# Chunked attention into a gated feed-forward layer on one core: idle products in the head, 32-row value loads, three more tiles transposed by DMA

## The chip, the core and the metric

The program runs on one core of one Trainium2 chip. The core has TensorE (PE: matrix products), VectorE (DVE), ScalarE (ACT), GpSimd (POOL) and SyncE (SP). In this kernel GpSimd issues nearly all loads, SyncE a few small loads and the transposing transfers, ScalarE the stores. The metric is the device time of one execution in microseconds; 248.0 is the median of three runs (247.66 to 248.37). "Span" is the profiled part of one execution.

## The reference

There are 4 batches, 8 heads, 768 positions, head dimension 64. Positions are taken in chunks of 32. The queries of a chunk see 8 memory keys of their head and the keys from 16 positions before the chunk to 8 after it:

```python
for c in range(nc):                       # nc = 24 chunks per batch
    l_start = max(0, c_start - 16); r_end = min(S, c_end + 8)
    k_full = concat([mem_k, k[:, :, l_start:r_end]]); v_full = concat([mem_v, v[...]])
    a = softmax(q_c @ k_full.T / sqrt(D))
    out[:, :, c_start:c_end] = a @ v_full
x = out.transpose(0, 2, 1, 3).reshape(B * S, H * D)      # 3072 x 512
y = (relu(x @ w_gate) * (x @ w_val)) @ w_out             # 512 -> 1536 -> 512
```

All inputs and the output are float32. The kernel casts in the loads and computes in 16-bit types with float32 sums.

## The kernel before

**Tiles and blocks.** A tile is 128 positions of one batch, all heads: 24 tiles, 6 per batch. Attention runs tile by tile. The feed-forward layer runs over blocks of tiles (`BLOCKS = [2, 2, 2, 4, 4, 4, 4, 2]`): a first layer of 12 chunks, each with a gate product `g_ps` and a value product `v_ps` (line 396; four matmuls of 128 x 128 by 128 x 256 or 512), a relu on ScalarE (line 402), a multiplication on VectorE into `gvT` (line 408), and then the out products (line 421), copied and stored by ScalarE.

**One attention tile.** q and k are loaded as bfloat16 and transposed: batch 0 as pairs of tiles from `qk_p` (line 225), later tiles by TensorE (line 264), and from tile `LATE_QK = 18` on by a transposing transfer that SyncE issues (line 272). TensorE's transposes end in PSUM and are copied to `qT` and `kT` by ScalarE or VectorE (lines 78 and 80). Then scores (line 298, 32 small matmuls), row maximum, subtraction, exponent, row sum, reciprocal and normalising (lines 311 to 341). The probabilities are transposed by TensorE (line 347) and copied, or, from tile `LATE_P = 18` on, by SyncE's transfers (line 351). The product with the values is line 370 for batch 0 and line 377 for the other batches, its result is copied to `xT`.

**Values.** In batch 0 the value rows are loaded in natural order (`v_n`) and shifted to chunk order by products with a band matrix (`vs_ps`, line 204), then copied into `v_q`, a part of `v_bd[0]`. From batch 1 on the values stand in `v_bd[b % 2]`, a tile with 128 partitions in which each chunk has 56 context rows and 8 memory rows for each of two halves, and zeros elsewhere. The zeros are four GpSimd memsets of 128 x 1536 words per set (line 129): set 1 early (`z 1`), set 0 after batch 0. Two loads per batch (line 173) bring 56 rows of each of 96 chunks, so that rows shared by neighbouring chunks are fetched twice; eight small transfers bring the memory rows (line 156).

**What sets the order.** The program is written out by a list scheduler at the end of the kernel (`schedule()`, lines 660 to 757): operations with a cost per engine, dependencies, priorities and buffer counts (`room`). It gives each engine a fixed order, which the chip then runs in order. Loads are issued in the order of the list `loads`. PSUM buffers are `fps` (4, feed-forward and shifts), `sps` (1, scores) and `aps` (2, transposes and attention outputs). The planner multiplies some TensorE costs by 1.8 before 20 us.

Of the kernel before, what the change touches and what calls it, by code (L numbers as in the profile page):

```python
# [9 lines left out]
F32 = mybir.dt.float32  # L10
F16 = mybir.dt.float16
BF16 = mybir.dt.bfloat16
# [7 lines left out]
def kernel(  # L20
# [12 lines left out]
    nc = tc.nc  # L33
# [42 lines left out]
    def copy(eng, o, i):  # L76
        if eng is nc.scalar:
            nc.scalar.copy(o, i)  # L78
        else:
            eng.tensor_copy(o, i)  # L80
# [14 lines left out]
    vmem_f = v_bd[1][:, HP - 1].rearrange("p c d -> p (c d)").bitcast(F32)[:, 0:HP * 2 * D].rearrange(  # L95
        "p (h d) -> p h d", h=HP)
    v_q = v_bd[0][:, 0:2].rearrange("p h c d -> p (h c d)").rearrange("p (h c d) -> p h c d", h=HP, d=D)
    v_n = {}
# [27 lines left out]
        )  # L126

    def zero(eng, t, hp):
        eng.memset(t[:, hp].rearrange("p c d -> p (c d)").bitcast(F32), 0.0)  # L129


    def mem_load():
# [37 lines left out]
    def load_v_rows(b, par, s0, s1, c0, c1):  # L170

        dst = v_bd[b % NSET].rearrange("p h c d -> p (h c) d")
        nc.gpsimd.dma_start(  # L173
            dst[64 * par + s0:64 * par + s1, c0:c1, D * par:D * par + D],
            bass.AP(tensor=v.tensor, offset=v[b, HP * par, 0, 0].offset + (CH * c0 + s0 - 16) * D,
                    ap=[[D, s1 - s0], [CH * D, c1 - c0], [1, D]]))

    def v_parts(b, par, c0, c1):
        parts = []
        if (b, par, c1) == (B - 1, 1, HP * NCH):  # L180
            c1 -= 1
            parts.append((b, par, 0, 48, c1, c1 + 1))
        return parts + [(b, par, 0, CTX, c0, c1)]


    def load_v_tile(t):
# [21 lines left out]
    def shift_copy(c0, eng):  # L208
        copy(eng, v_q[:, :, c0:c0 + 2, :].rearrange("p h c d -> p c h d"), TMP.pop(("sh", c0)))
# [292 lines left out]
    for a in range(NT):  # L502
# [41 lines left out]
        if b == 0:  # L544
            for c0 in (4 * t, 4 * t + 2):
                need = {c // 4 for c in (c0, c0 + 1)} | {max(c0 - 1, 0) // 4, min(c0 + 2, NCH - 1) // 4}
                gone = ([t - 1] if c0 % 4 == 0 and t else []) + ([t] if c0 == NCH - 2 else [])
                op(("sh", c0), {"PE": 0.4}, lambda e, c0=c0: shift(c0), [("vn", n) for n in sorted(need)] + ["ident"],
                   (1, a, 7.5), ["fps"], ["qk"] * len(gone), [("s", t)])
                op(("shc", c0), psum(2 * HP * D), lambda e, c0=c0: shift_copy(c0, engine[e]), [("sh", c0)],  # L550
                   (1, a, 7.6), (), ["fps"])
# [39 lines left out]
    def load_qk_op(a, i):  # L591
        load(("qk", a, i), 1024, 1.05, lambda: load_qk(a, i), take=["qk"])

    def load_v_op(b, half, par, c0, c1, n, deps, after):
        for i, part in enumerate(reversed(v_parts(b, par, c0, c1))):
            rows = part[3] - part[2]
            load(("vl", b, half, n) if i == 0 else ("vx", b, n), rows * (part[5] - part[4]),
                 rows * (part[5] - part[4]) * 1.15e-3, lambda part=part: load_v_rows(*part), deps, (), after)

    def load_w_op(g):  # L600
        for w in range(2):
# [1 line left out]
                load(("w", g, w, par), 256, 0.35 * (GROUPS[g][1] - GROUPS[g][0]), lambda g=g, w=w, par=par: load_gate_val(g, w, par))  # L603

    def load_zero(s, hp):
        load(("z", s, hp), 0, 1.5, lambda: zero(nc.gpsimd, v_bd[s], hp), ["vm0"] if s else [("v", TPB - 1)])

    def load_pair_op(r, i):
        load(("pl", r, i), 1024, 1.45, lambda: load_pair(r, i))
# [27 lines left out]
    for i in range(2):  # L637
        load(("wo", i), 768, 4.1, lambda i=i: load_out(i))
    for b in range(1, B):
        deps = [("z", b % NSET, HP - 1)] + ([("v", TPB * (b - NSET + 1) - 1)] if b > NSET else [])  # L640
        if b == 1:
            for n in range(2 * HP):
                op(("mr", b, n), {"SP": 0.72}, lambda e, n=n: mem_rows(nc.sync, 1, n),
                   deps + [(("vm", 0), 0.2), (("vm", 1), 0.2)], (0,))
        for par in range(2):
            load_v_op(b, 0, par, 0, HP * NCH, par, [], deps)
        if b > 1:
            for n in range(2 * HP):
                load(("mr", b, n), 192, 0.22, lambda b=b, n=n: mem_rows(nc.gpsimd, b, n),
                     deps + [(("vm", 0), 0.2), (("vm", 1), 0.2)])  # L650
        for a, i in late[5 if b == 1 else 9 + 12 * (b - 1):21 + 12 * (b - 1)]:
            load_qk_op(a, i)
        if b == 1:
            for hp in range(HP):
                load_zero(0, hp)

    def timed(d):
        return isinstance(d, tuple) and len(d) == 2 and isinstance(d[1], float)

    def schedule():  # L660
        done, started, times = {}, set(), [0.7]
        free = {e: 0.7 for e in ("PE", "ACT", "DVE", "SP", "POOL")}
        queue_end, flying, gives = 0.0, [], []
# [26 lines left out]
        while len(started) < len(ops) + len(loads):  # L690
# [8 lines left out]
            while moved:  # L699
                moved = False  # L700
                for e in ("POOL", "PE", "ACT", "DVE", "SP"):
# [18 lines left out]
                    else:  # L720
                        o = None
                        for _, key in todo[e]:
                            late_pe = e == "PE" and t > 36.0 and ops[key]["prio"][0] == 1
                            if ready(ops[key], t, MARGIN if late_pe else 0.0):
                                o = ops[key]
                                break
                        if o is None:
                            continue
# [62 lines left out]
```

## Time and profile before

| | |
|---|---|
| median of three runs | 248.0 us |
| the profiled execution | 247.81 us |
| its span | 246.0 us |
| TensorE busy | 233.3 us, 95% |
| VectorE, ScalarE, GpSimd busy | 132.7, 117.6, 90.6 us |
| first first-layer product | 22.24 us from the span's start |
| last out product ends | near 242.2 us |

How to read it. Times are microseconds from the start of the span. In an instruction row the columns are start, duration, engine, line, operation, output and inputs, count, and in brackets the idle time before it and what ended it. Matmuls overlap each other, so four that take 0.6 us in such a row stand closer than 0.15 us; the chain of waits counts from start to start. A row of the chain is start, duration and what the time was spent on; "issue" is time in which the engine waited for nothing that the profile names. "POOL DMA_DIRECT2D" is GpSimd writing the descriptors of a load, not the load itself; "landing" is when its data has arrived. The row PEclk is the TensorE clock that was granted, in tenths of full speed.

### The profile page before, as it was taken

To read this page: it belongs to the slowest core of one execution; us is meant where nothing else is said; L and a number is where in the kernel's file an instruction comes from. 1 tells how busy PE (TensorE), PEld (TensorE's weight loads), DVE (VectorE), ACT (ScalarE), POOL (GpSimd) and SP (SyncE) were. 2 spreads that over 40 slices of the span, in tenths; PEclk is the share of its full clock that TensorE was granted. 3 is DMA by queue.
4 is the path that set the end of the run, shared out by engine and by line. 5 is a ranking of instruction groups with operands and counts; after the bars stand their busy time and mean duration, and the time that the engine had idled before them with its cause. 6 is when DMAs were issued, how large, how long until landed. Compare 5 with 4: busy or idle time off the path is not lost.

```text
span 246.0 us, 6397 instructions
## 1 busy us (share of the span) xinstructions
PE 233.3 (95%) x2673; PEld 139.8 (57%) x2673; DVE 132.7 (54%) x260; ACT 117.6 (48%) x265; POOL 90.6 (37%) x105
## 2 busy tenths in 40 slices
PE   0869999999999999999999999999999999999994
PEld 0646887884488645555445545555445444444873
DVE  2372757984139748796048779999342034320430
ACT  2755867753275445643245575765332232312432
POOL 8965799813268991099921050000000000000000
PEclk9999999999999999999999999999999999999999
DMA  7999999999999899999999999671101210002102
GB/s 74 173 179 203 203 96 119 174 175 127 133 223 154 80 102 136 75 75 147 179 192 158 67 76 109 130 147 25 23 0 45 85 44 0 0 35 95 43 3 85
DMA packets 109757, 25.76 MB, mean 105 GB/s; under 512 B 100769, under 2 KB 106657, under 8 KB 109729
## 3 DMA queue, kind: packets, MB, share of 16 engines
q0 software_dynamic: 94368, 16.42, 107.7%
q1 hardware_dynamic: 11760, 2.64, 8.9%
q10 hardware_dynamic: 3600, 6.29, 7.9%
q8 instruction: 21, 0.34, 0.6%
q14 instruction: 8, 0.06, 0.1%
HBM read 32.06 MB, written 6.29 MB: 156 GB/s over the span
## 4 chain that ended last, share of the span: by engine, by line
PE 92%; DMA 2%; DVE 2%; issue 1%; ACT 1%; POOL 1%; ACTq 0%; POOLq 0%
PE v_ps L396 26%; PE g_ps L396 26%; PE out_ps L421 25%; PE xT_ps L377 3%; PE s_ps L298 3%; PE qk_ps L264 2%; DMA qk_p<-in_k_dram 2%; PE pT_ps L347 2%; PE xT_ps L370 2%; PE vs_ps L204 1%; PE qk_ps L225 1%; PE xT_ps L363 1%; DVE mx L311 1%; POOL qk_p L216 1%; DVE dif L318 1%
## 5 line engine op out<-in xcount | busy, mean ns | idle before, releaser
L408 DVE TENSOR_TENSOR gvT<-v_ps,g_relu 128x256 f16<-128x256 f32 (+1 forms) x96 | 53.0, 555 | 56.7 <-PE v_ps L396 41.0
L396 PE MATMUL g_ps<-xT,w_gate_sb 128*128 128x256 f16 (+1 forms) x384 | 78.5, 327 | 0.0
L396 PE MATMUL v_ps<-xT,w_val_sb 128*128 128x256 f16 (+1 forms) x384 | 78.2, 326 | 0.0
L402 ACT ACTIVATE g_relu<-g_ps 128x256 f16<-128x256 f32 (+1 forms) x96 | 46.9, 489 | 50.7 <-PE g_ps L396 50.0
L421 PE MATMUL out_ps<-w_out_sb,gvT 128*128 128x512 f16 (+2 forms) x300 | 65.7, 371 | 0.0
L396 PEld LDWEIGHTS <-w_gate_sb 128*128 128x128 f16 x384 | 36.4, 98 | 24.0 <-issue 0.4
L396 PEld LDWEIGHTS <-w_val_sb 128*128 128x128 f16 x384 | 35.9, 98 | 20.9 <-issue 0.2
L421 PEld LDWEIGHTS <-gvT 128*128 128x128 f16 x300 | 28.0, 98 | 29.9
L78 ACT COPY o_sb<-out_ps 128x512 f32<-128x512 f32 (+2 forms) x25 | 14.2, 567 | 37.2 <-PE out_ps L421 28.2
L326 ACT ACTIVATE p_exp<-dif 128x256 f16<-128x256 f32 (+2 forms) x72 | 19.5, 336 | 9.0 <-DVE dif L318 8.8
L243 POOL DMA_DIRECT2D qk_b<-in_k_dram x18 | 16.5, 915 | 15.0 <-issue 8.4
L311 DVE TENSOR_REDUCE mx<-s_ps 128x8 f32<-128x512 f32 x24 | 16.5, 688 | 8.3 <-PE s_ps L298 8.0
L156 POOL DMA_DIRECT2D v_bd<-vmem x16 | 10.1, 642 | 27.7 <-DMA v_bd<-in_v_dram 27.7
L330 DVE TENSOR_REDUCE sm<-p_exp 128x8 f32<-128x512 f16 x24 | 16.4, 682 | 6.0 <-ACT p_exp L326 5.9
L78 ACT CAST xT<-xT_ps 128x512 f16<-128x512 f32 x19 | 11.1, 584 | 15.4 <-PE xT_ps L377 10.2
L243 POOL DMA_DIRECT2D qk_b<-in_q_dram x18 | 16.4, 913 | 3.1 <-issue 2.0
L341 DVE TENSOR_TENSOR p_n<-p_exp,rinv 128x512 f16<-128x512 f16 x24 | 16.5, 687 | 0.4
L318 DVE TENSOR_TENSOR dif<-s_ps,mx 128x512 f32<-128x512 f32 x24 | 16.4, 684 | 0.4
L173 POOL DMA_DIRECT2D v_bd<-in_v_dram x7 | 14.0, 2015 | 1.0 <-POOL v_bd L129 0.6
L377 PEld LDWEIGHTS <-v_bd 128*128 128x128 f16 x288 | 9.6, 96 | 4.7 <-issue 1.1
L78 ACT COPY kT<-qk_ps 128x512 bf16<-128x512 bf16 x17 | 10.8, 641 | 2.9 <-PE qk_ps L225 1.9
L129 POOL MEMSET v_bd<- 128x1536 f32 x8 | 10.7, 1397 | 0.0
(52 smaller groups left out, 156.8 us busy)
## 6 DMA issues: line engine op xcount, KB each, us to landing
out_dram<-o_sb ACTq DMA_DIRECT2D x23, 256.0 KB
v_bd<-in_v_dram POOLq DMA_DIRECT2D x5, 672.0 KB, 17.6
qk_b<-in_k_dram POOLq DMA_DIRECT2D x18, 128.0 KB, 6.1
qk_b<-in_q_dram POOLq DMA_DIRECT2D x18, 128.0 KB, 6.4
w_out_sb<-in_moe_w_out_dram POOLq DMA_DIRECT2D x2, 768.0 KB, 11.2
qk_p<-in_k_dram POOLq DMA_DIRECT2D x3, 256.0 KB, 5.2
qk_p<-in_q_dram POOLq DMA_DIRECT2D x3, 256.0 KB, 7.1
v_n<-in_v_dram POOLq DMA_DIRECT2D x6, 128.0 KB, 6.5
```

Source lines behind the costliest of these rows:

```text
L78: nc.scalar.copy(o, i)
L243: nc.gpsimd.dma_start(qk_b[a, i], bass.AP(tensor=x.tensor, offset=x[b, 0, 128 * t, 0].offset, ap=[[D, 128], [S * D, H], [1, D]]))
L311: nc.vector.reduce_max(SM[a, "mx"], s4, axis=AX.X)
L318: nc.vector.tensor_tensor(out=SM[a, "dif"].rearrange("p (m r) a s -> p r m a s", r=2), in0=S_ps.pop(a).rearrange("p r (m a) s -> p r m a s ...
L326: nc.scalar.activation(p[:, :, :, s0:s0 + k1 - k0], dif[:, :, :, k0:k1], ACT.Exp, scale=SCALE)
L330: nc.vector.reduce_sum(SM[a, "sm"], SM[a, "p"], axis=AX.X)
L341: nc.vector.tensor_tensor(out=P_n[a], in0=SM.pop((a, "p")), in1=rinv_b, op=ALU.mult)
L377: nc.tensor.matmul(ps[:, hp, r], lhsT=v_bd[b % NSET][:, hp, 4 * t + g, :], rhs=x[:, hp, r], start=True, stop=True)
L396: nc.tensor.matmul(ps, lhsT=w[:, f, 128 * m:128 * m + 128], rhs=xTs[blk][:, f, :], start=(f == 0), stop=(f == NFC - 1))
L402: nc.scalar.activation(st["r", m], st.pop((0, m)), ACT.Relu)
L408: nc.vector.tensor_tensor(out=st["gv"][:, m, :], in0=st.pop((1, m)), in1=st.pop(("r", m)), op=ALU.mult)
L421: nc.tensor.matmul(st["o", t, c], lhsT=st["gv"][:, m, 128 * t:128 * t + 128], rhs=w_out_sb[:, m, c[0]:c[1]], start=(m == 0), stop=(m == ND ...
```

## The change

Four things are changed.

1. **Idle products.** VectorE zeroes a 128 x 128 tile `idle` first of all. Wherever the scheduler finds TensorE with nothing ready between 1.3 and 16 us of its own time, it puts a product of that tile with itself into TensorE's order; nothing reads the results, which go to one `fps` buffer that is given back at 16.1. The order has 61 of them before the first k transposes (25 before and 36 behind the kmem product), then 7, 5, 7 and 5 between the first transposes, 22 before the scores of tile 1 and 31 before the first transposes of q pair 1. The factor of 1.8 now ends at 8 us.
2. **Early zeros.** Set 1 of `v_bd` is zeroed in the head, three quarters by VectorE (one before and two behind the identity copies) and one by ScalarE, which copies from `idle`; GpSimd's four memsets between the loads go. The scratch `vmem_f` moves to set 0. The shift copies of tiles 0 and 1 are fixed to ScalarE.
3. **Value loads of 32 rows.** The two loads of a batch bring rows 0 to 31 of each chunk, and a load of 16 rows the end of the last chunk. The rows 32 to 55 are copied on VectorE from the next chunk's rows 0 to 23: 16 copies per batch (24 partitions x 12 or 11 chunks x 64), first half of the batch and second half apart. The values of a tile wait for them.
4. **Transposing transfers** start at tile 15 instead of 18, for q and k and for the probabilities.

```diff
+    UT = 3
-    LATE_QK, LATE_P = 18, 18
+    LATE_QK, LATE_P = 15, 15
...
+    idle = const.tile([128, 128], BF16, name="idle")
...
     def zero(eng, t, hp):
-        eng.memset(t[:, hp].rearrange("p c d -> p (c d)").bitcast(F32), 0.0)
+        x = t[:, hp].bitcast(F32)
+        if eng is nc.scalar:
+            z = idle.bitcast(F32)
+            nc.scalar.copy(x, bass.AP(tensor=z.tensor, offset=z.offset, ap=[z.ap[0], [0, NCH], [1, D]]))
+        else:
+            eng.memset(x.rearrange("p c d -> p (c d)"), 0.0)
+
+    def idle_product(N):
+        if "idle" not in TMP:
+            TMP["idle"] = fps.tile([128, 512], F32, tag="fps", name="idle_ps")
+        nc.tensor.matmul(TMP["idle"][:, 0:N], lhsT=idle, rhs=idle[:, 0:N], start=True, stop=True)
...
+    def upper(b, par, i0, i1, eng):
+        x = v_bd[b % NSET].rearrange("p h c d -> p (h c) d")
+        d = slice(D * par, D * par + D)
+        copy(eng, x[64 * par + CH:64 * par + CTX, i0:i1, d], x[64 * par:64 * par + CTX - CH, i0 + 1:i1 + 1, d])
...
+    op("idle", {"DVE": 0.2}, lambda e: nc.vector.memset(idle, 0.0), prio=(-10,))
+    for hp in range(HP):
+        op(("z1", hp), {"DVE": 1.5, "ACT": 1.6}, lambda e, hp=hp: zero(engine[e], v_bd[1], hp), ["idle"], prio=(-1, hp), after=["warm2", "vmem_f"] + ["ib"] * (hp > 0))
...
-           + ([("vl", b, 0, n) for n in range(2)] if b else [("shc", 4 * t), ("shc", 4 * t + 2), "vm0"])
+           + ([("vl", b, n) for n in range(2)] + [("up", b, n, m) for n in range(2 * HP) for m in range(t // UT + 1)]
+              + [("ve", b, n) for n in range(2) if last] if b else [("shc", 4 * t), ("shc", 4 * t + 2), "vm0"])
...
+    def load_v_op(b, par, deps):
+        n = HP * NCH
+        load(("vl", b, par), CH * n, CH * n * 1.03e-3, lambda: load_v_rows(b, par, 0, CH, 0, n), (), (), deps)
+        load(("ve", b, par), 16, 0.05, lambda: load_v_rows(b, par, CH, CH + 16, n - 1, n), (), (), deps)
...
-    for hp in range(HP):
-        load_zero(1, hp)
...
+                            if e == "PE" and 1.3 < t < WARM:
+                                order.append((t, lambda: idle_product(128)))
+                                free[e] = t + (0.107 if t < 6.0 else 0.056)
...
-                        d *= (1.8 if e == "PE" and t < 20.0 and key[0] in ("t", "p", "sh", "f") else 1.0)
+                        d *= (1.8 if e == "PE" and t < 8.0 and key[0] in ("t", "p", "sh", "f") else 1.0)
```

More of the change, by code (lines that the diff above doesn't have):

```diff
@@ L94 @@
     v_bd = [const.tile([128, HP, NCH, 2 * D], F16, name=f"v_bd_{s}") for s in range(NSET)]
-    vmem_f = v_bd[1][:, HP - 1].rearrange("p c d -> p (c d)").bitcast(F32)[:, 0:HP * 2 * D].rearrange(
+    vmem_f = v_bd[0][:, HP - 1].rearrange("p c d -> p (c d)").bitcast(F32)[:, 0:HP * 2 * D].rearrange(
         "p (h d) -> p h d", h=HP)
@@ L592, in load_qk_op @@
         load(("qk", a, i), 1024, 1.05, lambda: load_qk(a, i), take=["qk"])
[L594 to L598, printed above, removed]
+    def load_v_op(b, par, deps):
+        n = HP * NCH
+        load(("vl", b, par), CH * n, CH * n * 1.03e-3, lambda: load_v_rows(b, par, 0, CH, 0, n), (), (), deps)
+        load(("ve", b, par), 16, 0.05, lambda: load_v_rows(b, par, CH, CH + 16, n - 1, n), (), (), deps)
+    for b in range(1, B):
+        for n in range(2 * HP):
+            hp, par = divmod(n, 2)
+            for m in range(TPB // UT):
+                i0 = NCH * hp + 4 * UT * m
+                i1 = min(i0 + 4 * UT, HP * NCH - 1)
+                op(("up", b, n, m), {"DVE": 0.1 + 64 * 0.5e-3 * (i1 - i0)},
+                   lambda e, b=b, par=par, i0=i0, i1=i1: upper(b, par, i0, i1, engine[e]),
+                   [("vl", b, par)], (1, TPB * b - 1 + 3 * m, 9) if b > 1 else (1, TPB * b - 1 + UT * m, -1), (), (), [("v", TPB * b - 7)] if b > 1 else [])
     def load_w_op(g):
@@ L605, in load_zero @@
     def load_zero(s, hp):
-        load(("z", s, hp), 0, 1.5, lambda: zero(nc.gpsimd, v_bd[s], hp), ["vm0"] if s else [("v", TPB - 1)])
+        load(("z", s, hp), 0, 1.5, lambda: zero(nc.gpsimd, v_bd[s], hp), [("v", TPB - 1)])
     def load_pair_op(r, i):
@@ L639 @@
     for b in range(1, B):
-        deps = [("z", b % NSET, HP - 1)] + ([("v", TPB * (b - NSET + 1) - 1)] if b > NSET else [])
+        deps = ([("z", 0, HP - 1)] if b > 1 else [("z1", hp) for hp in range(HP)]) + ([("v", TPB * (b - NSET + 1) - 1)] if b > NSET else [])
         if b == 1:
@@ L655 @@
                 load_zero(0, hp)
+    HASTE, WARM = 0.0, 16.0
     def timed(d):
@@ L662, in schedule @@
         free = {e: 0.7 for e in ("PE", "ACT", "DVE", "SP", "POOL")}
-        queue_end, flying, gives = 0.0, [], []
+        queue_end, flying, gives = 0.0, [], [(WARM + 0.1, "fps")]
+        room["fps"] -= 1
+        heapq.heappush(times, WARM + 0.1)
         todo = {e: [] for e in free}
@@ L726, in schedule @@
                                 break
+                            alone = len(ops[key]["eng"]) == 1 or e == "ACT"
+                            if e != "PE" and 6.0 < t < HASTE and alone and ready(ops[key], t + 0.4):
+                                break
                         if o is None:
+                            if e == "PE" and 1.3 < t < WARM:
+                                order.append((t, lambda: idle_product(128)))
+                                free[e] = t + (0.107 if t < 6.0 else 0.056)
+                                heapq.heappush(times, free[e])
+                            elif e == "PE" and t <= 1.3:
+                                heapq.heappush(times, 1.31)
                             continue
```

10 lines of the change are left out of this document (2 added, 8 removed).

## The prediction

> **What bounds the kernel now.** I read the page's busy times and slices first, then TensorE's instructions in order of time, then the chain of waits.
>
> ```profile
> span 246.0 us, 6397 instructions
> PE 233.3 (95%) x2673; PEld 139.8 (57%) x2673; DVE 132.7 (54%) x260; ACT 117.6 (48%) x265; POOL 90.6 (37%) x105
> ...
> PE   0869999999999999999999999999999999999994
> ...
> PEclk9999999999999999999999999999999999999999
> ...
> PE 92%; DMA 2%; DVE 2%; issue 1%; ACT 1%; POOL 1%; ACTq 0%; POOLq 0%
> ```
>
> TensorE is full from the third slice to the last. A gain is work taken off it, or an earlier start of that full stretch. The granted clock reads full everywhere, so TensorE's real rate must be read from durations:
>
> ```profile
> 12.42 1.49 PE L204 MATMUL vs_ps<-v_n,band 128*64 128x256 f16 x12
> 15.35 0.61 PE L347 MATMUL pT_ps<-band,p_n 128*128 128x128 f16 x4 [1.43 <-DVE p_n L341]
> 16.62 0.59 PE L363 MATMUL xT_ps<-pT,vmem 128*128 128x128 f16 x4 [0.67 <-ACT pT L78]
> 22.24 1.03 PE L396 MATMUL g_ps<-xT,w_gate_sb 128*128 128x256 f16 x4
> 23.55 1.36 PE L204 MATMUL vs_ps<-v_n,band 128*64 128x256 f16 x12
> 24.75 0.39 PE L225 MATMUL qk_ps<-ident_b,qk_p 128*64 128x128 bf16 x8
> 25.07 0.61 PE L396 MATMUL v_ps<-xT,w_val_sb 128*128 128x256 f16 x4
> ```
>
> Four 128x256 products took 1.03 us at 22.24 and 0.61 us at 25.07: until about 24.6 TensorE runs at half rate, though it was almost always busy from 6.2 to 13.9. The Trainium skill, "TensorE: Matmul & The Clock Gate", Part 1, says about 3.4 us of sustained matmuls open the gate; the trace disagrees, for those small products and transposes did not. Its Part 4, that transposes do not count as busy, agrees.
>
> ```profile
> 63.83 3.25 PE out_ps L421 x15
> 67.08 0.66 issue
> 67.74 1.06 PE xT_ps L377 x32
> ...
> 124.91 0.45 PE qk_ps L264 x8
> ...
> 144.07 0.22 PE qk_ps L264 x4
> ```
>
> This is the chain of waits: TensorE's costs from start to start, and its one pause after the head, 0.66 us before the values of tiles 6 and 7. The second v load of that batch was issued at 43.9 and landed 23.6 us later, at 67.5: it ended that pause.
>
> ```profile
> 84.22 2.21 POOL L173 DMA_DIRECT2D v_bd<-in_v_dram  x1 [0.57 <-POOL v_bd L129]
> 84.69 1.90 DVE L252 COPY kT<-kmemT 128x768 bf16<-128x768 bf16 x1
> 137.55 0.31 DVE L252 COPY kT<-kmemT 128x768 bf16<-128x768 bf16 x1
> ```
>
> The same VectorE copy took 0.31 us with GpSimd idle and 1.90 us under a GpSimd load, ending 0.16 us after it. Such copies are what the change adds.
>
> **The change, part by part.**
>
> *Idle products.* Nothing in the trace is a product of zeros; the nearest rows are the 128x128 products of L347: four in 0.61 us cold, one lasting 0.307, so 0.10 apart; four in 0.39 warm, so 0.055 apart. 61 stand before the first transposes: 25 (2.5 us from about 1.1) end before the kmem product at 4.21; 36 follow from 4.7 and end at 6.7 if the clock opens at once, 8.3 if it does not. The first k pair landed at 6.20, so they cost 0.5 to 2.1 us there; I take the middle, 7.2. From there to the scores of tile 0 lie one transpose group (0.6) and four ScalarE copies (0.66 each): about 10.5 against 9.71. The later products (7, 5, 7, 5, 22, 31) fill pauses; warm, 22 take 1.2 us and 31 take 1.7, beside the max-subtract-exp chain of 2.2 and 3.4 us, and are hidden; cold they would not be.
>
> *What ends the head then.* The order puts the first transposes of q pair 1 before P's transpose of tile 0. That load was issued at 9.76 and landed 7.1 to 7.6 us later; I take 17.2, a wait of TensorE that takes the place of the 1.43 us one. Behind it: transposes 0.28, P 0.39, VectorE's copy 0.42 (17.2 to 18.3); tile 0's second copy and values 0.83 (19.3); tile 1's reciprocal, normalise, P, copy beside these (20.3); values 0.83, ScalarE's copy 0.6 and the k transposes 0.57 beside it: the first-layer product starts at about 22.3. Before, it started at 22.31. But by then after has also done the scores (0.24), 12 shifts (0.78) and 8 transposes (0.22) that before did later: 1.24 us. And it meets no cold rows: before paid 0.53 extra for g (0.97 less 0.44), 0.10 for scores, 0.51 for the shifts (1.29 less 0.78): 1.14. Bounds for the start: 21.5 (landing 16.9, no waits between) to 23.3.
>
> *Dense start.* ScalarE must now give up four shift copies (0.59 each), k copies (0.64) and the first relus in the 4 us around the start, where cold TensorE used to leave time; the four fps buffers empty no faster. I charge 1.0 us (0 to 2).
>
> *Early zeros.* Two 128x1536 memsets follow ident_b on VectorE at 4.27. From the 128x512 row (0.485) each is at most 1.46, so the kT copy behind them ends at 7.5, or 9.1 if it waits like the 1.90 row. Scores at 10.5 cover it. ScalarE's zero (at most 3 x 0.584 = 1.75, from 2.24) ends before its 4.72 copy. If GpSimd's v loads are held up behind the memsets by up to 2.9 us, the DMA backlog (k landed at 9.1, first v at 10.05) hides most; the second v tile then costs up to 1 us, in the slack before 17.2. Price 0. On GpSimd 5.35 us of memsets go, and every load behind them is issued earlier.
>
> *Transposing transfers for tiles 15 to 17.* Six q/k groups of 0.22 and three P groups of 0.22 leave TensorE: 2.0 us. A following 128x512 group reads 0.97 instead of 0.86 after such a switch; about five switches fewer, 0.5. Together 2.5 (bounds 2.0 and 3.0). SyncE issues nine more, 1.2 to 1.9 us each, all behind its first at 112.77, before which it had waited 59.7 us: hidden. Its k_t copies replace PSUM copies of the same size (0.62 for 0.64 on ScalarE): no charge.
>
> *32-row v loads and copies.* Each load shrinks to 32/56. Before, the second landed 8.5 us after the first; at that ratio 4.9, and the first 3.1 instead of 5.4 behind w_out (landed 53.6). The five q/k loads ahead come about 3.1 us earlier (tile 8's k landed at 44.4; 35.5, the end of the backlog, plus 0.5 and five at 1.05 is 41.3). So the second v load lands near 53.6 - 3.1 + 3.1 + 4.9 = 58.5. Four copies then stand before tile 6's values: 0.31 each if free, 1.2 each if each waits for a 0.9 us GpSimd load: ready at 59.7 to 63.3. TensorE reaches these values after 24 out products, earlier than before: 22.3 + 31.3 (48 first-layer groups 20.9, scores 1.0, shifts 2.2, P and transposes 2.1, values 3.3, switches 1.8) + 6.1 (24 x 0.216, transposes, P, scores) + 1.0 above = 60.7. I take 61.5, a pause of 0.8 (0 to 2.6) for the 0.66 that goes. For batch 2, 16 copies join VectorE, busy 16.8 of 20 us from 90 to 110; I charge 0.4 (0 to 3). Batch 3's stand beside out products that need no VectorE. Behind a copy that waits for its load stand the gates; batch 2's and 3's loads come earlier than before, since GpSimd waited for v landings up to 67.5 and 104.3.
>
> The Trainium skill, "SBUF — State Buffer", section "SBUF: two separate sides", speaks against this part: a two-port VectorE operation and a GpSimd one exclude each other for a whole instruction. The 1.90 us row agrees. By it all copies beside loads cost 1.2 us, which is the third rival below.
>
> **The sum.** From 22.31 on, before spends 246.0 - 22.31 = 223.7 us. Take off 0.66, 1.14, 1.24 and 2.5: 218.1. After: 22.3 + 218.1 + 1.0 + 0.8 + 0.4 = 242.6 of span. Around the span lay 247.81 - 246.0 = 1.8 us; the profiled run lay 0.2 under the median of 248.0. Forecast: 244.4.
>
> **The rivals.**
>
> 1. *The added waits are all hidden.* For it: VectorE was busy only 3.8 of 12.3 us from 55.3 to 67.6. Then 22.3 + 218.1 + 1.8 = 242.2.
> 2. *The clock falls back when the idle products end,* in the 1.7 us pause before 17.2 and the thin work behind it, which in before never opened it. Price: values 2 x 0.8, shifts 0.6, k transposes 0.6 cold, then the 1.14 again, less the 1.0 of dense start: +2.9, 247.3, no change. Against it: after 24.6 no row slows again, though no pause there is longer than 0.66. By the clock page's rule only an idle window of about 3.4 us closes the gate, which would exclude this.
> 3. *Copies wait for GpSimd each time.* Tile 6's values wait 2.6 us, and 16 copies at 1.2 are 19 us of VectorE in a stretch with some 5 us to spare, so gates run late by about 3 us. 244.4 - 1.2 + 5.6 = 248.8, slower. It decides from about 0.9 us a copy. Against: loads are issued in bursts, and the 0.31 row.
> 4. *The change does not do what it says: products of zeros do not open the clock.* Then 36 cost 3.6 us, 22 and 31 cost 2.2 and 3.1 us cold, in the chain: scores at 11.7, P 10.5 us later at 22.2, first layer 7 us behind that (15.35 to 22.31 before) at 29.2. Plus 218.1 + 1.14 + 1.8: 250.2. Against it: a dense product is the only thing new just before 24.6.
>
> **How the numbers follow.** Forecast 0.53, rivals 0.22, 0.11, 0.08, 0.06. The forecast's own case covers 243 to 246. Range 241.7 to 248.2, leaving out the slow tails of 3 and 4 and a start below 22. A measurement of this kernel tells about 0.3% (0.7 us) from no change. Faster: 0.53 + 0.22 + a quarter of the second rival = 0.78; within: the rest of it, 0.08; slower 0.14.
>
> **What would show it.** Right: 0.055 us between idle products from about 6 to 8 us; 12 shifts in about 0.8 us before 16; a TensorE wait for q's load ending near 17.2; first-layer product near 22.3 at 0.61 for four; out products beginning near 54.5; values of tile 6 after a wait of under 1.5 us; the end at 240 to 244 of span. Wrong: 1.0 us for the first four 128x256 products, VectorE copies of 0.9 us or more before tile 6, a TensorE wait on gvT around 85 to 125, or waits for weights (w_val of chunk 6 landed near 29.7, needed at about 30.7).

## The result and the profile after

The changed kernel takes 254.92 us (median of four runs, 253.16 to 255.39); the kernel before took 248.19 in the same comparison. The ratio is 1.0264, 95% interval 1.0235 to 1.0293: slower by 2.6%. The forecast was 244.4 with a range of 241.7 to 248.2, so it had the wrong sign. (Ratios below leave out slow executions, one each of e4, e10 and e11 and four of ten of e9; of e8 five of six were slow, so it has no ratio, and the profiles of e8, e9 and e10 show slow executions.)

The page of the changed kernel, its busy times, slices and the shares of the chain of waits:

```profile
span 253.6 us, 6674 instructions
PE 240.0 (95%) x2775; PEld 145.8 (58%) x2775; DVE 160.1 (63%) x312; ACT 116.9 (46%) x260; POOL 83.1 (33%) x106
...
PE   7988799998929999999999999999999999999995
...
PEclk9999999999986999999999999999999999999999
...
PE 89%; DVE 3%; ACT 3%; issue 2%; DMA 1%; SPq 0%; ACTq 0%
```

A slice is 6.3 us. In the twelfth TensorE is nearly idle (2), and in it and the next the granted clock is down (8 and 6 tenths). The kernel before had neither. The instructions of that stretch, in order of time (start, duration, engine, line, operation, count, and in brackets the idle time before):

```profile
67.49 0.90 POOL L254 DMA_DIRECT2D qk_b<-in_k_dram  x1
67.83 6.12 DVE L81 COPY v_bd<-v_bd 24x768 f16<-24x768 f16 x1
68.35 5.38 POOL L136 MEMSET v_bd<- 128x1536 f32 x4
...
69.01 1.47 PE L432 MATMUL out_ps<-w_out_sb,gvT 128*128 128x512 f16 x6
73.98 0.20 DVE L345 RECIPROCAL rinv<-sm 128x8 f32<-128x8 f32 x1
...
74.60 0.69 DVE L352 TENSOR_TENSOR p_n<-p_exp,rinv 128x512 f16<-128x512 f16 x1
...
75.35 0.61 PE L358 MATMUL pT_ps<-band,p_n 128*128 128x128 f16 x4 [4.87 <-DVE p_n L352]
...
77.03 1.06 PE L407 MATMUL g_ps<-xT,w_gate_sb 128*128 128x256 f16 x4
...
80.84 0.60 PE L407 MATMUL v_ps<-xT,w_val_sb 128*128 128x256 f16 x4
```

One of the new copies, which takes 0.35 us as a rule, takes 6.12. It begins beside a GpSimd load (67.49 to 68.39) and ends at 73.95, 0.2 us after the four zeros of set 0 on GpSimd. Queued behind it on VectorE are the reciprocal and the normalising of tile 7, and TensorE's next instruction is the transpose of that `p_n`: it stands still for 4.87 us. When it goes on, four 128x256 products take 1.06 us, and at 80.84 again 0.60. The granted clock says the same. Columns of the next rows: stretch, its length, busy time and count of TensorE, its weight loads, VectorE, ScalarE and GpSimd, then the granted clock, DMA share and GB/s.

```profile
72.00:74.00 2.00, 0.00 (x0) 0.00 (x0) 1.97 (x2) 0.00 (x0) 1.73 (x2) 0.99 0.78 170
74.00:76.00 2.00, 0.65 (x5) 0.55 (x6) 1.90 (x5) 0.01 (x1) 1.97 (x3) 0.50 0.57 96
76.00:78.00 2.00, 2.00 (x9) 1.00 (x8) 0.62 (x1) 1.39 (x4) 2.00 (x3) 0.50 1.35 94
78.00:80.00 2.00, 2.00 (x29) 1.73 (x28) 1.12 (x3) 1.45 (x3) 2.00 (x4) 0.50 2.01 149
80.00:82.00 2.00, 2.00 (x18) 1.65 (x16) 1.55 (x4) 1.05 (x3) 0.35 (x2) 0.80 3.15 127
```

From 75.35 to about 80.8 TensorE runs at half rate, which costs some 2.7 us on top of the 4.87. Together that is 7.6. That the span grew by the same 7.6 (253.6 less 246.0) is chance, for the other parts of the change gain something (e1 below). The same four zeros were in the kernel before, where TensorE did not wait for them:

```profile
78.30 5.35 POOL L129 MEMSET v_bd<- 128x1536 f32 x4
```

They now run ten us earlier. The lighter loads ahead of them account for most of that: with loads of 56 rows and all else changed (e9) the zeros begin at 75.07.

In the head the changed kernel has these rows, before and at the first transposes of k, and one later stall:

```profile
4.87 4.04 PE L141 MATMUL idle_ps<-idle 128*128 128x128 bf16 x36
8.84 0.75 PE L236 MATMUL qk_ps<-ident_b,qk_p 128*64 128x128 bf16 x16
...
28.44 0.62 PE L215 MATMUL vs_ps<-v_n,band 128*64 128x256 f16 x7 [1.31 <-issue]
```

The 36 products stood 0.11 apart and held up k, which had landed at 6.2, until 8.84. The first first-layer product came at 24.96, where the forecast had 22.3; in the kernel before, with less work ahead of it, it came at 22.24. The stall of 1.31 has no cause that the profile names; more on it below.

### The profile page after: what moved, and what is told of

Same layout as the page of the kernel before. It is cut to its first block, busy times and chain, and to the rows that moved or that the text cites. A ratio compares the mean times of both kernels' runs of the same rounds, so it can differ in the third digit from the quotient of the medians.

```text
span 253.6 us, 6674 instructions
## 1 busy us (share of the span) xinstructions
PE 240.0 (95%) x2775; PEld 145.8 (58%) x2775; DVE 160.1 (63%) x312; ACT 116.9 (46%) x260; POOL 83.1 (33%) x106
## 4 chain that ended last, share of the span: by engine, by line
PE 89%; DVE 3%; ACT 3%; issue 2%; DMA 1%; SPq 0%; ACTq 0%
PE v_ps L407 25%; PE g_ps L407 25%; PE out_ps L432 23%; PE idle_ps L141 3%; PE xT_ps L388 3%; DVE v_bd L81 3%; PE s_ps L309 2%; PE vs_ps L215 2%; PE pT_ps L358 2%; PE qk_ps L236 2%; PE qk_ps L275 1%; PE xT_ps L381 1%; DMA kmem_f<-in_mem_k_dram 1%; ACT kT L79 1%; PE xT_ps L374 1%
## 5 line engine op out<-in xcount | busy, mean ns | idle before, releaser
L432 PE MATMUL out_ps<-w_out_sb,gvT 128*128 128x512 f16 (+2 forms) x300 | 66.8, 373 | 0.8 <-issue 0.8
L81 DVE COPY v_bd<-v_bd 24x768 f16<-24x768 f16 (+1 forms) x48 | 24.1, 546 | 0.6
L329 DVE TENSOR_TENSOR dif<-s_ps,mx 128x512 f32<-128x512 f32 x24 | 16.4, 683 | 0.3
L185 POOL DMA_DIRECT2D v_bd<-in_v_dram x12 | 11.1, 936 | 11.9 <-PE xT_ps L388 11.6
L141 PE MATMUL idle_ps<-idle 128*128 128x128 bf16 x138 | 12.2, 260 | 1.0 <-DVE warm L471 1.0
L168 POOL DMA_DIRECT2D v_bd<-vmem x16 | 10.2, 652 | 8.5 <-DMA v_bd<-in_v_dram 8.2
L141 PEld LDWEIGHTS <-idle 128*128 128x128 bf16 x138 | 10.8, 120 | 1.7 <-DVE warm L471 1.0
```

The source lines that it names most:

```text
L141: nc.tensor.matmul(TMP["idle"][:, 0:N], lhsT=idle, rhs=idle[:, 0:N], start=True, stop=True)
L432: nc.tensor.matmul(st["o", t, c], lhsT=st["gv"][:, m, 128 * t:128 * t + 128], rhs=w_out_sb[:, m, c[0]:c[1]], start=(m == 0), stop=(m == ND ...
```

## Experiments

"Before" is 248.1 to 248.2 us in all comparisons. Ratios are to it, with 95% intervals.

### The copy and the zeros

Theory: VectorE's copy and GpSimd's memsets shut each other out, and the wait and the fall of the clock follow from that. Rivals: the copy waited for data; the head is to blame.

**e1: the zeros of set 0 behind the last copy of batch 1.** A tiny GpSimd copy that reads the last rows written makes them wait:

```diff
+    def zero_behind(s, hp):
+        if hp == 0:
+            nc.gpsimd.tensor_copy(fence[96:97, 0:1], v_bd[1][96:97, HP - 1, 4 * UT, 64:65])
+        zero(nc.gpsimd, v_bd[s], hp)
```

> The change with one small GpSimd copy put ahead of the four zeros of set 0; it reads the last rows that the last copy of batch 1 writes, so the zeros cannot start before that copy has ended. Theory (lock): VectorE's copy and GpSimd's zeros shut each other out, and the copy that began at 67.83 waited for all four zeros. Then no copy of batch 1 takes over 1 us, the wait of 4.9 us at the transposes of p goes, the granted clock stays at 1.00 between 74 and 82, and the time falls by 4.9 + 2.7 to 247.3 (246 to 249). Rival (data): the copy waited for rows of v still landing, or for something else than the zeros; then it still takes some 6 us and the time stays at 254.9. Rival (products): the loss comes from the head; then the time stays within 1 us of 254.9 although the copy is short.

246.47 us (244.89 to 247.63), ratio 0.9925 [0.9898, 0.9952]: 8.45 us less than the change, and 0.75% faster than before. The instructions on VectorE and GpSimd:

```profile
66.47 0.74 DVE L81 COPY v_bd<-v_bd 24x768 f16<-24x768 f16 x1
67.24 0.20 DVE L346 RECIPROCAL rinv<-sm 128x8 f32<-128x8 f32 x1
67.47 0.35 DVE L81 COPY v_bd<-v_bd 24x704 f16<-24x704 f16 x1
...
67.97 0.63 POOL L635 COPY fence<-v_bd 1x1 f16<-1x1 f16 x1 [0.94 <-DVE v_bd L81]
68.66 5.33 POOL L137 MEMSET v_bd<- 128x1536 f32 x4
...
70.68 0.42 DVE L81 COPY qT<-qk_ps 128x512 bf16<-128x512 bf16 x1 [0.80 <-PE qk_ps L276]
71.02 0.68 DVE L342 TENSOR_REDUCE sm<-p_exp 128x8 f32<-128x512 f16 x1
...
72.17 0.69 DVE L353 TENSOR_TENSOR p_n<-p_exp,rinv 128x512 f16<-128x512 f16 x1
```

The zeros start only 0.3 us later than in the change and are as long, but the longest of the 48 copies is now 0.88 us, no wait at 70 is left, and the granted clock is 1.00 from 68 to 84. While the zeros run, VectorE's copy out of PSUM, its sum and its two-input product keep their usual 0.42, 0.68 and 0.69. The one form seen shut out by them is the 16-bit copy from SBUF to SBUF. The theory holds, and both rivals fall.

**e4: the same zeros in quarters, at the place where the change has them.**

```diff
-            eng.memset(x.rearrange("p c d -> p (c d)"), 0.0)
+            for i in range(4):        # on GpSimd
+                eng.memset(x[:, w * i:w * i + w], 0.0)
```

> The change with each of the four zeros of set 0 cut into four memsets of a quarter of the size, 16 in a row, in the same place. If VectorE's copy gets in between two GpSimd instructions (lock by the instruction), it takes at most 0.5 to 0.8 us and the time falls to about 247.3. If the copy waits until GpSimd's whole run of memsets is over (lock by the run), it takes some 6 us again and the time stays at 254.9. If the wait had nothing to do with the memsets, it also stays, with the copy ending at another point than the memsets.

247.61 us, nine of ten runs from 246.0 to 249.1 and one at 254.8. This did not decide: in the profiled execution GpSimd had issued its loads half a us later, and of the last copies (67.47 for 0.75 and 68.48 for 0.61) one was through and one had begun when the zeros began at 68.86. The one run of 254.8, which has no trace, looks like the collision.

**e5: twelve useless memsets of GpSimd in one run among the ten copies of batch 1** (on top of e1), so that they must meet:

```diff
+        if (a, i) == (2 * TPB, 1):
+            for w in 2 * list(qk_p.values()):
+                nc.gpsimd.memset(w.rearrange("p h d -> p (h d)").bitcast(F32), 0.0)
```

> The kernel with the zeros behind the last copy, and beside that twelve useless memsets of 128x512 f32 (into the six tiles of batch 0's loads, each twice; they are dead by then) on GpSimd, in one run, ahead of the load of tile 12's k, so that they begin near 59, among the ten copies of batch 1 on VectorE that ran from 57.4 to 61.2. By the 1.34 us of 128x1536 f32, one of them takes 0.45 and the run 5.4. Lock by the instruction: copies and memsets take turns, no copy takes over 0.35 + 0.45 = 0.8, and the ten end by 66 at the latest. Lock by the run: one copy takes over 4 us and ends with the last memset. No lock (the wait of 6.12 in the change had another cause): all copies keep their 0.35 to 0.75.

251.0 us (two runs). The two engines, and TensorE behind them:

```profile
56.07 9.45 DVE L81 COPY v_bd<-v_bd 24x768 f16<-24x768 f16 x10
...
57.86 0.87 POOL L258 DMA_DIRECT2D qk_b<-in_q_dram  x1 [3.37 <-DMA v_bd<-in_v_dram]
58.73 5.67 POOL L256 MEMSET qk_p<- 128x512 f32 x12
...
64.67 0.53 PE L392 MATMUL xT_ps<-pT,v_bd 128*128 128x32 f16 x8 [2.63 <-DVE v_bd L81]
```

The copies of this batch alone (count: shortest/median/longest in ns, first and last start):

```profile
L81 DVE COPY v_bd<-v_bd x16: 341/352/6541, 56.1 to 70.5; 24x768 f16<-24x768 f16 x14, 24x704 f16<-24x704 f16 x2
```

The copy that began at 58.1, beside the load, took 6.54 us and ended at 64.6, 0.2 us after the last of the twelve memsets. In eleven changes from one memset to the next it did not get in. So the lock holds for the run, not for the instruction. The records leave no gap for it: each memset is recorded for 0.54 us, yet the twelve take only 5.67, so each begins before the one ahead of it has ended. With DMA issues it is mostly another matter: in e1 GpSimd issued loads without a pause from 58.1 to 67.0, and ten copies from 57.37 on took 3.87 us together. A copy of e1 that began in the first 0.2 us of a load kept its 0.35; one that began 0.2 to 0.5 us into it took 0.45 to 0.88, until 0.15 to 0.19 us after that load's end.

### The products on zeros

**e2: the products left out, all else in the same order. e3: that, and e1.**

```diff
-                                order.append((t, lambda: idle_product(128)))
```

> The change with its products on zeros left out, and every other instruction in the same order. Theory (head): the 36 cold products in front of the first transposes of k delay them from 6.7 to 8.8 and the delay is handed on, while the clock that they open gives back less; then the first layer starts at 22.3 instead of 24.96, and the time falls by up to 2.6 to 252.3; the 4.9 us wait at 70 stays. Rival (products pay): without them the small matmuls run at half rate until 24 and the first layer starts at 25 or later; the time is 254.9 or above, up to 256.

> Both edits: zeros behind the last copy, and no products on zeros. If the lock costs 7.6 and the products 2.6, the time is 244.7; if the products pay for themselves, 247.3 or somewhat more; if neither theory holds, 254.9.

e2 takes 255.19 us (ratio 1.0266 [1.0222, 1.0309]), as the change does, with a wait of 6.4 us for `p_n` in place of 4.9. It shows the lock a third time: a copy of 7.91 us that began at 64.46 beside a load, stayed out through two more loads and the four zeros, and ended 0.2 us after these. e3 takes 246.18 (0.9919 [0.9891, 0.9946]), as e1 does. All the products together are worth nothing either way, so neither theory of e2 was right. They do open the clock early: in e1 the eight transposes at 8.82 take 0.41, in e3 those of 9.19 take 0.64, and the first layer starts at 24.04 and at 25.27. But what they gain is lost again in stalls, which no kernel without products shows in its first 60 us. These are e1's:

```profile
14.91 0.22 PE L310 MATMUL s_ps<-kT,qT 64*32 64x64 bf16 x7 [0.57 <-issue]
...
21.38 0.25 PE L310 MATMUL s_ps<-kT,qT 64*32 64x64 bf16 x14 [0.60 <-issue]
...
27.52 0.62 PE L216 MATMUL vs_ps<-v_n,band 128*64 128x256 f16 x7 [1.31 <-issue]
...
59.19 0.39 PE L433 MATMUL out_ps<-w_out_sb,gvT 128*128 128x512 f16 x1 [0.29 <-issue]
```

**e10 and e12: e1 with 54 products (25 and 29), or 35 (25 and 10), and none behind the first transposes of k.**

```diff
-                                order.append((t, lambda: idle_product(128)))
+                                if t < 6.7:                      # e12: 5.2
+                                    order.append((t, lambda: idle_product(128)))
```

> The kernel with the zeros behind the last copy, with 54 products on zeros in place of 138: 25 ahead of the first transposes of mem_k, 29 behind them, and none after the first transposes of k. Theory (feed): in the kernel with all products TensorE stood still, with nothing in the profile that it waited for, behind matmul 223, 351, 478 and 987, for 0.57, 0.60, 1.31 and 0.29 us, 2.8 in all; the same places in all four kernels with products, 128, 127 and 4 x 127 matmuls apart, and nowhere in those without products; so it waits for its own instructions when it runs through many short ones. With 84 products fewer it has less to fetch, the stalls shrink, and the time falls to between 243.7 and 245.5. Rival (the clock shuts): without later products the granted rate of the small matmuls falls back before 20, the stalls go but eight transposes take 0.64 again in place of 0.41, and the time stays at 246.2 (246 to 246.6).

> The same with 35 products (25 and 10), which end at 5.6, before k lands at 6.2. If the products opened the clock only near 7 (when 54 or more had run), it does not open here, the sixteen transposes of k take 1.06 as without products, and the time is 246.2 as in the kernel without products. If the clock opens all the same, k is transposed from 6.3 in place of 7.6 and the time is up to 1 us below the run with 54.

e12 takes 249.03 us (1.0036 [1.0009, 1.0064]), e10 250.25 in the median of five of its six executions (1.0096 [1.0058, 1.0133]); in the profiled one, 305 us, the granted clock did not go above 0.75 from 10.2 on. Both are slower than with all products and than with none. In e12 the clock opened near 8.2. e12 then had a pause of 2.70 us before the transposes of 16.58:

```profile
12.00:14.00 2.00, 1.29 (x44) 0.87 (x44) 1.22 (x3) 1.83 (x6) 2.00 (x4) 1.00 1.51 197
14.00:16.00 2.00, 0.00 (x0) 0.00 (x0) 1.93 (x4) 1.48 (x5) 1.86 (x4) 0.76 1.81 177
16.00:18.00 2.00, 1.18 (x12) 0.87 (x13) 0.90 (x2) 0.73 (x1) 0.62 (x1) 0.50 2.23 163
```

So the clock shut, as the rival has it; with the 22 and 31 later products, which the forecast called hidden fillers, it stayed open here in e1. But that is not what makes e12 slower than e3, which has the same order without products. Here are the same instructions in e3,

```profile
53.49 0.61 PE L408 MATMUL g_ps<-xT,w_gate_sb 128*128 128x256 f16 x4
...
58.51 0.39 PE L359 MATMUL pT_ps<-band,p_n 128*128 128x128 f16 x4
```

and in e12:

```profile
53.30 0.61 PE L408 MATMUL g_ps<-xT,w_gate_sb 128*128 128x256 f16 x4
...
57.60 0.28 PE L408 MATMUL v_ps<-xT,w_val_sb 128*128 128x256 f16 x1 [2.49 <-issue]
...
60.98 0.39 PE L359 MATMUL pT_ps<-band,p_n 128*128 128x128 f16 x4
```

At 53.30 e12 is 0.19 us ahead, although its clock had shut. Then one stall of 2.49 us, where its own count of matmuls stands at 859, puts it 2.47 behind, and the spans end 2.5 apart (246.6 and 244.1). Fewer products made fewer stalls, but in this execution not less stalled time: one of 2.49 us with 35 products, four of 2.77 together with 138 in e1.

### The transposing transfers

**e7: e1 with LATE 18. e8: the kernel before with LATE 15 alone. e11 and e17: e3 with LATE 12 for both, or for q and k alone.**

```diff
-    LATE_QK, LATE_P = 15, 15
+    LATE_QK, LATE_P = 18, 18      # e7;   e8: 15, 15;   e11: 12, 12;   e17: 12, 15
```

> The kernel with the zeros behind the last copy, and tiles 15 to 17 transposed by TensorE as before (LATE_QK and LATE_P 18). The forecast priced the transposing transfers at -2.5 (2.0 to 3.0): then this is 246.47 + 2.5 = 249.0. If the transfers' gain is lost again elsewhere, 246.5.

> The kernel before with LATE_QK and LATE_P 15 alone. By the same price 248.2 - 2.5 = 245.7 (245.2 to 246.2). If the transfers come in the way of the loads that are in the air in batch 2, or their landings are late, 248 or more.

> The kernel with the zeros behind the last copy and no products, with LATE_QK and LATE_P 12: three more tiles are transposed by transfers. If a tile is worth what tiles 15 to 17 are by measurement ((248.26 - 246.47) / 3 = 0.6 us each), 246.2 - 1.8 = 244.4. If these transfers meet the loads of v of batch 2, which run from 74 to 95, as those of the kernel with LATE 15 alone met the loads of batch 3 (landing 13 us after issue), a wait of over 3 us for pT or kT appears between 85 and 125 and the time is above 247.

> The kernel with the zeros behind the last copy and no products, with LATE_QK 12 and LATE_P 15: q and k of tiles 12 to 14 are transposed by transfers, their probabilities by TensorE. In the kernel with both at 12 TensorE waited 7.5 us for transfers of p. If it is the transfers of p alone that are late (they stand in the chain of a tile, those of q and k are planned ahead), no such wait is left here and six groups of 0.22 us leave TensorE: 246.2 - 1.3 = 244.9 (244.5 to 245.5). If the transfers of q and k are late as well, or hold up SyncE's queue, a wait for kT, qT or pT of over 2 us stays and the time is above 246.5.

e7 takes 248.26 us (1.0016 [0.9993, 1.0039]), so the transfers of tiles 15 to 17 are worth some 2 us in e1 (1.8 by the medians, 2.3 by the ratios). Alone in the kernel before they cost: e8 takes 252.66 in the fastest of six executions, 4.6 more than before, and 257.25 in the median. Its loads of v for batch 3, the first transfer of p and the values that need it:

```profile
118.63 2.23 POOL L173 DMA_DIRECT2D v_bd<-in_v_dram  x1 [1.03 <-issue]
125.33 2.78 POOL L173 DMA_DIRECT2D v_bd<-in_v_dram  x2 [4.47 <-issue]
...
141.49 25.51 SPq L351 DMA_TRANSPOSE pT<-p_n  x5
...
154.87 0.59 PE L377 MATMUL xT_ps<-pT,v_bd 128*128 128x32 f16 x16 [7.23 <-DMA pT<-p_n]
```

The transfer was issued at 141.49 and landed 13.3 us later. From 140 to 150 the DMA share was 3.2; in e1, whose 32-row loads of batch 3 were issued at 108.0 and were through, it was below 0.3 from 130 to 150, and no values waited for a transfer. After its wait e8 also ran at half rate, from 154.9 to 160.

With three more tiles the transfers meet loads again, though these bring only 32 rows: e11 takes 254.92 (1.0253 [1.0210, 1.0296]) and waits four times for p, 7.5 us in all. Leaving p to TensorE (e17) helps but does not cure: 249.57 (1.0059 [1.0020, 1.0098]). Its chain of waits contains a transfer of k and one of p:

```profile
98.66 8.67 DMA k_t<-qk_b
...
128.59 8.59 DMA pT<-p_n
```

So transfers of q and k are late too, and in these runs the forecast's price for a transfer, TensorE's time saved, held only in e1, where no loads were in flight beside the transfers of p.

### The loads of 32 rows, the early zeros, the order of the head

**e9: the change with the loads of v as before, without copies. e16: the kernel before with the 32-row loads and copies alone** (and set 0's zeros behind the last copy). The diff is e9's; e16 puts into the kernel before what e9 takes out of the change. (What is expected below and above speaks of loads of 48 rows; the kernel before loads 56 rows of each chunk, as the kernel's description has it, and 48 only of the last one.)

```diff
-           + ([("vl", b, n) for n in range(2)] + [("up", b, n, m) for n in range(2 * HP) for m in range(t // UT + 1)]
-              + [("ve", b, n) for n in range(2) if last] if b else [("shc", 4 * t), ("shc", 4 * t + 2), "vm0"])
+           + ([("vl", b, 0, n) for n in range(2)] if b else [("shc", 4 * t), ("shc", 4 * t + 2), "vm0"])
...
-        load(("vl", b, par), CH * n, CH * n * 1.03e-3, lambda: load_v_rows(b, par, 0, CH, 0, n), (), (), deps)
+            load(("vl", b, half, n) if i == 0 else ("vx", b, n), rows * (part[5] - part[4]),
+                 rows * (part[5] - part[4]) * 1.15e-3, lambda part=part: load_v_rows(*part), deps, (), after)
```

> The change with the v loads of 48 rows as before and without the copies; products, early zeros and transfers from tile 15 stay. The zeros of set 0 stay where the change has them. Theory (lock): without copies there is nothing for the zeros to shut out, so the 4.9 us wait goes, the clock stays open and the time is 246 to 247.5 (246.5 of the repaired change, plus the 0.66 us wait for v). Rival (zeros too early, whatever stands beside them): some wait of over 3 us at 68 to 75 stays and the time is above 250.

> The kernel before with the 32-row loads of v and their copies alone (and the zeros of set 0 behind the last copy): set 1 is zeroed by GpSimd at its old place, nothing is transposed by transfers ahead of tile 18, no products. By the forecast this part gives 0.66 and costs 0.8 + 0.4: 248.2 + 0.5 = 248.7 (247.5 to 251). If the lighter queue is worth more than that, it is below 247.5.

e16: 248.79 us (1.0021 [0.9997, 1.0044]), 0.1 from what the forecast's terms give, and not clear of no change. e9: 251.69 in the median of all ten, 1.0087 [1.0055, 1.0120] by the ratio, which is 250.3. No wait at 68 to 75 is left in it, as the lock theory has it, but its zeros run only from 75.07 on, so it says little against the rival. It is not at 246 to 247.5: in the profiled execution the longest wait is one of 4.75 us at 150.04 for a transfer of p, as in e8. The lighter loads carry the transfers; alone they give nothing.

**e13: e3 with the zeros of set 1 on GpSimd at their old place. e14: e1 without products and with an order planned without them** (no PSUM buffer held back for them, and the shift copies of tiles 0 and 1 again free to go to either engine).

```diff
+    for hp in range(HP):                                     # e13, behind load_v_nat(5)
+        load(("z1", hp), 0, 1.5, lambda hp=hp: zero(nc.gpsimd, v_bd[1], hp))
...
-                            if e == "PE" and 1.3 < t < WARM:  # e14; factor 1.8 until 20 us again
-                                order.append((t, lambda: idle_product(128)))
```

> The kernel with the zeros behind the last copy and no products, with the zeros of set 1 by GpSimd at their old place (four memsets behind the sixth load of v_n), not by VectorE and ScalarE in the head. The forecast priced the move of the zeros at 0 in the head and at 0.66 us of earlier v loads: then this is 246.2 + 0 to 0.7, so 246.2 to 246.9. If the early zeros hold up VectorE's first work in the head (vmem 7.6 in place of 6.4), this is faster than 246.2, by up to 1 us.

> The kernel with the zeros behind the last copy, without products, and now also with the order that the planner writes when it knows of none (its factor of 1.8 back to 20 us, no buffer held back). In the kernel whose products were only left out of the finished order, TensorE had some 1.1 us less done by 30 us than the kernel before, although nothing stood in its way. Theory (order): that loss lies in the head's order, which was planned around the products; then this kernel starts its first layer before 24 and takes 245.1 (244.6 to 245.6). Rival (zeros, copies): the loss comes from the other parts, and the time stays at 246.2.

e13 takes 248.94 us (1.0035 [1.0011, 1.0059]): the early zeros are worth 2.8 us, not 0 to 0.7. Without them GpSimd's first load for batch 1 comes at 35.5 in place of 30.2 and the loads of v at 41.6 in place of 37.6, and between 100 and 120 TensorE is idle for 1.0 us, in e3 for 0.15. Another 0.65 is there when the first layer starts (25.92 in place of 25.27); the rest is not located. e14 takes 246.81 (0.9946 [0.9921, 0.9971]); its first layer starts at 24.74. So it is not the products' place in the order that keeps the first layer from starting at 22.3. Most of the difference to the kernel before is work moved ahead of it: the change, e3 and e14 all do 32 score products, 12 shifts and 8 transposes ahead of the first layer that before did behind its start, and these take some 2.3 us in e3, whose clock is not open yet. That leaves 0.7 of the 3.0 us between e3 and before, and its cause is open.

## Why the prediction was wrong

- **The step that failed** is the price of a copy beside GpSimd: "0.31 each if free, 1.2 each if each waits for a 0.9 us GpSimd load", and "a pause of 0.8 (0 to 2.6)". The row under it, a copy of 1.90 us beside a load, was the right row. But the bound was taken from one load. The longest work of GpSimd, the four zeros of 5.35 us at 78.30 in the page of before, was never held against the copies. Measured: one copy of 6.12 us, in e2 7.91, in e5 6.54, and without it 8.45 us less (e1). The values of tile 6 had no pause at all; tile 7's `p_n`, which the forecast did not name, was what stood behind that copy.
- "**Batch 2's and 3's loads come earlier than before**" was booked as a gain. By the same step the zeros came ten us earlier, from behind the copies into them.
- **What a long wait costs** was missing: a rate of one half for 5.5 us behind it. The second rival had the mechanism, but in the head, where it did not happen in the change; the clock stayed open from 9.1 to 74.0. It did happen in the heads of e12 and e4. What the prediction held against this rival, that only a longer idle stretch closes the gate, did not hold: in e12 a pause of 2.70 us was enough.
- **The third rival** ("copies wait for GpSimd each time", 248.8) had the right partner and the wrong form: copies that began in the middle of a load did wait for its end, but took 0.45 to 0.88 in e1, not 1.2, the others 0.35, and one copy beside a run of memsets cost more than all of this rival's waits together (5.6).
- **The fourth rival** fell: products on zeros do open the clock (in the change 31 of them took 1.90 us and 22 took 1.40, 0.056 apart). They are not the only way, against what the prediction read from the profile of before: in e16, which has none, four transposes of p took 0.40 at 15.37, against 0.61 in before, and the clock fell to 0.50 again at 16.4.
- **Idle products.** The first transposes of k were forecast at 7.2 (6.7 to 8.3; the middle of these would be 7.5). They came at 8.84, and with the same order ahead of them at 7.58 in e1 and 6.54 in e5: the moment of opening differs between executions. The later products do lie beside waits for other engines, as forecast. The 1.14 us of cold rows that they were to save came back as stalls, 2.77 us in e1, a term that the sum does not have: e1 and e3 are equal.
- **What ends the head.** In the change q pair 1 was not waited for; the first layer started at 24.96, not 22.3, and in e3 without products at 25.27. This term is wrong by 2.7. Of these, 1.7 are there at P's transpose of tile 0, forecast to begin at 17.5: it came at 19.22, right behind its `p_n`, because tile 0's scores began at 12.50, not 10.5, after the late transposes of k. In e3 this step was right: TensorE waited 1.59 us for q pair 1, to 16.93, and P's transpose came at 17.50. Behind P lay 5.7 us in the change, not the forecast's 4.8, and 7.8 in e3; why is only in part seen (0.33 in the change is a stall).
- **Early zeros** at 0: too low in gain, e13 shows 2.8.
- **Transposing transfers** at -2.5 (2.0 to 3.0): -1.8 to -2.3 measured, and "hidden" on the condition that the v loads of the batch are through; without that +4.6 or more (e8).
- **32-row loads with copies** at +0.54 net: +0.5 measured (-0.1 to 1.1, e16), apart from the lock.
- **The sum.** With the lock taken out (e1) the time is 246.47, 2.1 above the forecast and 1.7 below before. The sign was lost by one term. That e1 lies in the forecast's range is in part luck: the late first layer and the stalls, which the sum lacks, stand against the early zeros, which it priced at nothing. What the parts measure (-2, -2.8, +0.5, 0) does not add up to -1.7 either, for each was measured beside the others.

## What to carry to other kernels

Whoever adds SBUF-to-SBUF copies on VectorE looks through the page for the longest unbroken run of GpSimd's own work, not for its longest instruction, and asks where that run stands after the change: a faster queue moves it. It costs little to fix its place by a true dependency. And a wait of TensorE is to be priced with the half-rate stretch behind it, a transfer with the queue that it meets, not with the work it saves, and filler products on TensorE with the stalls that more instructions can bring.

## What the runs showed of the hardware that was not expected

- **The lock lasts for GpSimd's whole run.** The Trainium skill, "SBUF — State Buffer", section "SBUF: two separate sides", says that whichever of the two starts first holds the shared ports for the whole instruction. Here a copy waited through 4 memsets in a row (6.12 us, and 7.91 in e2) and through 12 (6.54 us). That it began beside a load in all three cases may matter; a copy that met a memset from idle was not tried.
- **The clock falls after short pauses.** The granted clock went to 0.50 in or behind pauses of 2.63 (e5), 2.70 (e12 and e11), 3.02 (e11), 4.75, 4.87, 6.35 and 7.23 us, and not behind those of 1.31 (e1), 2.29 (e17) and 2.49 (e12, at 57.6). In e4 it fell at 23.2 with no pause ahead of it longer than 0.87, so the length of one pause does not decide alone. The stretches at 0.50 lasted 3.4 us (e4, e5, e11 twice), 6.8 (the change, e2, e9) or 10.2 (e8, e12): one, two or three times 3.41. The Trainium skill, "TensorE: Matmul & The Clock Gate", Part 1, gives an idle window of about 3.4 us; the pauses up to 3.02 here were shorter.
- **TensorE stops at fixed counts of matmuls.** In the six kernels with the full products the stalls without a named cause stand behind the same matmuls, by the traced count 223 and 351 (all six), 478 (not in e4) and 987 (not in e5 and e9): 128, 127 and 509, or about 4 x 127, apart (some records are missing from a trace). The page of the changed kernel lists the instruction stream as

```profile
q8 instruction: 22, 0.36, 0.7%
```

  which is 22 packets of some 16 KB. An estimate from this: 128 matmuls, each with a weight load, are 256 instructions, which would fill such a packet at 64 bytes each. The traces bear it out: all 22 stalls of this kind in seven traces, e12's with them, end 1.2 to 1.9 us after one of these packets has landed. The packet ahead of e12's stall took 2.13 us (53.54 to 55.67), those of its first 50 us 0.9 to 1.0. So TensorE very likely waited for its next instructions; no experiment moved them.
